# A hand-tuned list schedule made anew: another load pace, another bias between two engines, another set of nudges

## The chip, the cores and the metric

The kernel runs on one core of a Trainium2 chip. Its time is device microseconds of one execution; five executions of the kernel before took between 175.0 and 175.97 us, with a median of 175.41. The core has five engines that run side by side and wait for each other through semaphores: PE multiplies matrices into PSUM banks, DVE and ACT do elementwise work and empty the banks, POOL issues the loads, and SP issues stores, small copies and transposes by DMA.

## What is computed

Attention over four batches of eight heads, 768 positions and 64 columns a head, is followed by a gated long convolution over the same 512 channels:

```python
scores = scale * np.matmul(q, k.transpose(0, 1, 3, 2)) + bias   # local window of 96, 8 global keys
a = softmax(scores);  x = concat_heads(a @ v)                   # (4, 768, 512)
proj = x @ w_proj;  x1, x2, x3 = split(proj, 3)
x2_conv = irfft(rfft(x2) * rfft(filter_fft))                    # over the 768 positions
out = (x1 * x2_conv * x3) @ w_out                               # (4, 768, 512) float32
```

## The kernel before

Each batch goes through two halves. In the attention half, q and k tiles are transposed on PE (`transposes`, or `transpose_pair` for batch 0), `scores` multiplies them for a pair of heads, ACT takes the exponential, DVE multiplies by a mask, `values` multiplies by v, DVE divides by the row sums (the tile `xn`), and `transpose_x` brings the result to `xT` with channels on partitions. For batch 3, q and k are transposed by DMA on SP instead (the set `CROSS`). In the convolution half, `butterfly` forms sums on DVE, `conv` projects them on PE (L1168) into `ab`, `forward` transforms them (L921) into `X`, DVE multiplies by the filter's spectrum (`prod`, `sums`), and PE transforms back (L1190, L1193) into `eo`. `mixed` and `gated` on DVE make `y` from it and from `gate` (L1107, which multiplies `xT` by the outer columns of `w_proj`), and `project` (L1224) multiplies by `w_out`; the tile `ot` is stored. Attention of batch b+1 runs beside the convolution of batch b.

The code does not write the order of the work by hand. Every operation is recorded in a `Plan` with its cost in microseconds per engine, the values that it reads and writes, and the PSUM banks that it takes. `lay` then walks a clock of its own: at each step it takes, among the operations that are ready, the one that can start first, with a rank that decides between near ties. The rank is the operation's due time in its batch plus a nudge from the list `NUDGES`, which holds two numbers for each operation in the order of recording: the first is added to the rank (hundredths), the second to a lean (thousandths). Where an operation may run on ACT or on DVE, it goes to the engine on which it would end first, with `FAVOUR` plus the lean added on DVE's side. Copies that empty a PSUM bank (`evac`, `copy`, `times`) have this choice; masks, `prod`, `mixed` and `gated` are DVE's alone, exponentials ACT's.

Loads are costed in two parts: the issue on POOL, from the count of packets (L581), and the transfer, which the plan sends through a serial queue of POOL loads, `n * cost / 16` for n packets, so that a later load lands after all earlier ones. `load_run` loads the value tiles of batch 0, one DMA per tile; `load_rows`, `load_q` and `load_v` load those of the other batches.

Where PE would stand still, `fill` puts matmuls on a zero tile (`busy`, L561). `program` at last hands each engine its operations in the planned order. Each engine then runs its own list in that order and waits where an input is not there. The plan's times are gone by then: only the order and the choice of engine remain.

Of the kernel before, what the change touches and what calls it, by code (L numbers as in the profile page):

```python
# [16 lines left out]
P = 128  # L17
NG = 8
KL = P - NG
# [45 lines left out]
class Plan:  # L65
# [90 lines left out]
    def lay(self):  # L156
# [84 lines left out]
        20941, -23817, 24195, -7663, -15997, -12768, 0, 6867, 24904, -5965, 0, -17644, -7477, -5060, -24645,  # L241
        7853, -19816, -5063, -21771, 2690, -43764, -11197, -12559, 13745, -25952, 704, 42886, 22331, -9503,
        -5990, 1975, -8514, 0, -4745, 0, -11122, 0, -4678, 0, -2503, 0, 2703, 49094, -5453, 12582, 138, 0,
        2677, 0, -19674, 0, 1176, -15359, 22897, 0, -11534, 10311, -526, -2410, -3266, -17322, 33944, 3602,
        1512, -259, 8045, -40045, 7265, 30354, -27115, -43002, 18207, -23341, -7539, -18530, 19032, 26814,
        -11634, -11666, 14102, -46374, 23798, -33916, -1835, -50116, 19804, 11572, 3115, -29987, 8167,
        28348, 11218, -36506, -4010, 22595, 36152, -34543, -29090, 14477, 8599, -2614, 27869, 0, -7546, 0,
        -16680, 0, -17125, 0, -13816, 0, -16742, 0, -14791, 0, 16347, 0, 25926, 0, -5843, 0, 4323, 0, 10329,
        0, -15463, 0, 18719, 19536, 1819, 15033, -8513, 19843, -16154, 22937, -10325, 10268, 18083, 28464,
        -245, 36921, 25314, 18091, 23717, 29990, 35772, 38801, 14920, -6087, 48142, 8522, 52890, 26449,  # L250
        9945, 19818, 13034, -4027, 31031, 38806, 4230, 41538, 37058, 57207, 5161, 73250, 47340, 15138, 7448,
        7588, -18862, -23184, 16201, 32855, -3461, -31158, 19212, 17292, -17171, -42089, 23948, -22897,
        41474, 22968, 9803, 20589, 17748, 27185, 9614, -12894, 18131, 34936, 25299, 8438, 6083, -14729,
        -6326, 20819, -4821, -45272, 14951, 23049, 18994, 19751, 14180, 9780, 8132, -5251, 30597, 5195,
        -13743, -20605, 22464, -8378, 9715, -15388, 24239, 30711, -28388, -18939, -10787, -61348, 4309,
        -55267, -13, 1094, 47816, -21137, 19514, -30248, 2935, -8278, -9837, -18023, -6570, 60379, 10396,
        -16481, -3595, 36204, 6725, 7341, 2733, -6320, 2309, -25178, -24402, -13811, 32179, -16072, 9119,
        -2714, 7410, 3663, 9827, -12105, 12955, -28897, -10780, 51012, 14628, 1754, -22401, 13485, -3085,
        -4184, -21186, 36085, 6397, -8855, 31954, -12447, -8150, 15733, -13896, 5026, 16795, 39884, -2708,
        -12411, 41445, 7799, -26420, -28275, -1112, 280, 15059, -34598, 7843, 11808, -2433, -42337, -15655,  # L260
        -82713, -26014, -2215, 17107, -16388, 8416, -5143, -482, 11676, 33336, -33050, -14302, -15709, 144,
        -40429, 16554, 20320, -15285, -23321, -23667, -37185, -1273, -54080, -28453, -27659, 6317, -22336,
        19053, 19920, -9468, 13332, 22411, 27116, 4391, -74445, 3023, -18681, -23979, -41613, 4865, 40148,
        7658, 30769, -27204, 74556, 7934, 45890, 33096, 13491, -38443, -29399, 22140, -31839, 3648, 16007,
        9481, -16106, 20874, 29238, 150, 21929, 13455, 55399, 11501, -15951, 23586, -26638, -4060, 43304,
        -15855, -14976, -24332, -29525, 11042, -20570, 17346, -12584, -16297, -2377, 13286, -4899, -10436,
        -16741, -11712, -11582, 3253, -26673, 7977, -2469, -30454, -20346, 4897, -20954, -22758, -46710,
        10239, -64392, 12875, 21717, 11446, -5702, -21422, -30610, 8795, -40918, -18411, -67424, -18195,
        -69743, -37254, -9433, 5562, -19751, -18453, -71731, -18388, -70805, -1711, -10582, -11961, -23871,
        -19336, -40186, 22987, -5316, -14258, -16870, -14629, -15256, -1521, -23735, -47928, 16443, 10761,  # L270
        54821, -14436, 72922, 14379, 51678, -16015, 7320, -29070, 46924, -8772, 32829, -16584, 31588, -6267,
        34457, 3590, -31558, 24732, -10923, -14504, 32964, 8385, 5143, 36919, -32728, 25956, -14039, 11349,
        4986, 12927, 31546, 37533, -59658, -3559, 18051, 38808, 73841, -2119, 50706, 31457, 23261, -6025,
        -10079, 16467, 30400, 21292, 8455, 18584, -31806, 7305, 57789, 8768, 50111, 13745, -35470, -3712,
        41732, 25577, 24126, 19787, 8533, -937, 21590, 18777, 39119, 2282, -20749, -8396, 12672, 28818,
        16646, -10937, 11614, -10567, -21879, 2676, 18819, 31186, 4639, -15944, 16046, -32624, -29674, 1458,
        -9769, 13249, 0, 5375, 0, 1092, 0, 12535, 0, -19918, 0, 7960, 29554, -1962, 0, -31760, -168, -6234,
        32766, -9812, 0, -10387, 0, -9046, 0, -15969, 0, -982, 0, 14749, 0, 3802, 0, -1279, 0, 787, 0,
        24394, 0, 585, 0, -8398, 0, -11228, 0, 3326, 0, 6490, 0, 8805, -9920, 48938, 4735, 3905, -8205,
        -7191, -2044, 30228, 9924, 17307, 44468, -7542, -13358, -26667, -32913, -1805, -12682, 11399, 4538,  # L280
        3723, -22628, -3325, -5518, -17717, -21936, -17617, 10761, 26253, 20517, 7433, -4870, 28624, 25658,
        19340, 26925, -2699, 6125, 1356, -32310, 4183, -34292, 9989, -301, 1810, -17428, 15687, 23847,
        -22689, 26981, -20480, 46983, 12123, 9766, -4520, -746, 28862, 34014, 10760, 6990, 8399, -5341,
        -15584, 1444, -14598, -73642, 3303, 13007, 8220, -28684, 28385, 13493, 24628, -45198, -17244,
        -10136, 9475, -47887, -7547, 7854, 3939, -42446, 4154, 6812, 8242, -48704, -1611, -63875, 33975,
        -7810, -11179, -28621, 16046, -44155, 9482, 11839, 816, 25833, -4109, -14570, -12788, -4638, -2226,
        38013, -10513, -15011, -22283, -13043, -4434, 42230, -3028, 22311, -8443, -17844, 235, 18709, 7407,
        694, 17699, -24403, -29271, 4023, 6438, 43047, 1961, -12567, -29992, -8533, -4997, 40320, 27143,
        -1596, 11862, -21869, 8088, 32138, 44960, -6503, 17127, -15964, -21900, 21021, 59471, -34643, 12523,
        -54582, -1316, 4600, 20558, -6800, 9656, -21248, 21127, -32577, -23524, -12065, 10079, 7711, 11366,  # L290
        -17248, 26917, -25081, 12272, -16114, 12346, -3728, -4335, 21426, -10974, -27771, -20579, -13097,
        17282, -13589, -356, 22677, -15422, -10715, -12729, -34376, 2982, -20468, 11300, 2568, 7069, -5522,
        31878, -34399, -7695, 40664, -13553, -2045, -23324, -3339, -14404, -30632, -16381, -30178, 40050,
        -5959, -18941, 65029, -12040, 5363, 12421, -38116, -914, -35103, -4066, -4341, -20161, 26164,
        -21963, -9873, 21957, -2405, -6671, -20834, -12785, -47639, 27815, -8119, -1028, -4099, -31470,
        -45086, -17747, -56282, -14506, -37669, -8628, -5599, -35946, 1030, -12669, -35647, -2384, -32701,
        5577, 11677, -18878, 19540, -2288, -3689, 3395, -22559, -3163, -53669, -13281, 12767, -23778, 2008,
        -11131, 17587, -6082, -27729, 3930, -34024, 15838, 7012, -4139, 5154, -18748, -10652, -14438,
        -38218, -7406, -27281, 3651, 8333, 2357, 4397, -10262, -10115, 15008, -19298, -2425, -4559, 12746,
        -19302, -12587, 20081, 15257, -15456, -670, -12979, -20565, -7481, -4642, 9549, -23538, 42477, 921,  # L300
        -33191, 5231, 23254, -26129, -25207, -20621, -36661, 31925, -8000, 22268, -22467, -11797, -11838,
        -23754, -59344, 27973, -19506, -27508, -61395, 25876, 15950, -5301, -31395, -19472, 15820, -2929,
        -1351, -4676, 11568, -5649, 12795, -20002, 15116, -21404, -1438, 419, 26641, 2392, -5098, -775,
# [83 lines left out]
        -47616, 6427, 4471, 18429, -13169, 10884, -52679, -25140, 13532, 17369, 12295, -1454, 22421, -26080,  # L387
        22521, 13223, -4166, 12199, -22498, 6019, 50773, -19701, 32853, 1141,
    )
    FAVOUR = 0.0  # L390

    def fill(self, out):

# [75 lines left out]
class Fused:  # L469
# [458 lines left out]
    def transposes(self, what, t, src, cols):  # L928

        nc, g = self.nc, self.g  # L930
        b = g.bank()
# [494 lines left out]
```

## Time and profile before

| | |
|---|---|
| median of five executions | 175.41 us |
| profiled execution, span and own time | 173.2 us, 175.0 us |
| PE busy | 163.6 us, 1727 matmuls, 27 of them fillers |
| DVE, ACT busy | 148.7 us, 149.8 us |
| POOL busy | 75.5 us, all before 88 us |
| clock granted to PE | 1.00 throughout |
| first matmul of the values | 16.93 us, the second 17.67 us |
| last matmuls (outputs) start | 164.03 us |

The span runs from the first to the last instruction; the profiled execution's own time lies 1.8 us above it. In a row of the timeline the first number is the start, the second the time from the start of the first to the end of the last instruction merged into it; the part in brackets is how long the engine stood idle before it, and for what. The busy time of a matmul includes its way through the array, so that neighbours overlap: sixteen matmuls of 384 columns take 2.60 us from one start to the next group's, while each is shown as 0.33.

### The profile page before, as it was taken

The numbers are of one execution on the slowest core, as the hardware profiler recorded it, in microseconds if no ns is written. First come the engines' busy times: TensorE is split into PE (matmuls) and PEld (weight loads), VectorE is DVE, ScalarE is ACT, GpSimd is POOL, SyncE is SP. The second block draws the span as 40 slices with busy tenths as digits, with TensorE's granted clock in tenths as the row PEclk, the third lists the DMA queues.
The fourth block names the chain that finished last, engine by engine and source line by source line (L and its number), as shares of the span: only waits on it lengthen the run. The fifth ranks groups of instructions, "written<-read, shape, count | busy, mean of one in ns | idle before, by whom it ended". The sixth has DMA issues, their size and how long they took to land.

```text
span 173.2 us, 4484 instructions
## 1 busy us (share of the span) xinstructions
PE 163.6 (94%) x1727; PEld 101.7 (59%) x1727; DVE 148.7 (86%) x360; ACT 149.8 (86%) x298; POOL 75.5 (44%) x97
## 2 busy tenths in 40 slices
PE   7798999978999999999999999999999999999991
PEld 2376767645445656876445667754556784466540
DVE  6543869889999987999998999899999999999930
ACT  7999997976999986999998996889999797878761
POOL 7999777287997998799920000000000000000000
PEclk9999999999999999999999999999999999999999
DMA  6999999999999999999999994300431000040354
GB/s 180 159 126 124 112 184 207 188 153 151 138 148 167 150 154 149 114 143 151 142 128 93 364 149 95 61 0 0 192 114 62 4 0 2 0 184 2 140 222 185
DMA packets 86997, 21.82 MB, mean 126 GB/s; under 512 B 77616, under 2 KB 84032, under 8 KB 86976
## 3 DMA queue, kind: packets, MB, share of 16 engines
q0 software_dynamic: 75408, 12.47, 111.0%
q1 hardware_dynamic: 11568, 9.07, 19.8%
q8 instruction: 13, 0.21, 0.5%
q14 instruction: 8, 0.07, 0.1%
HBM read 25.69 MB, written 6.29 MB: 185 GB/s over the span
## 4 chain that ended last, share of the span: by engine, by line
PE 72%; DMA 13%; POOL 5%; DVE 4%; ACT 3%; issue 1%; POOLq 0%; ACTq 0%
PE bank L1107 19%; PE bank L1224 12%; PE bank L1168 12%; DMA qn<-in_q_dram 9%; PE bank L921 6%; PE bank L1190 5%; PE bank L984 5%; DMA vn<-in_v_dram 4%; PE bank L1069 3%; PE bank L1024 3%; PE bank L935 3%; PE bank L1029 2%; ACT E L999 2%; DVE xn L1048 2%; POOL kn L581 1%
## 5 line engine op out<-in xcount | busy, mean ns | idle before, releaser
L1107 PE MATMUL bank<-xT,w 128*128 128x384 f16 x256 | 45.7, 326 | 0.0
L999 ACT ACTIVATE E<-bank 128x864 f16<-128x864 f32 x48 | 41.3, 933 | 0.7 <-PE bank L984 0.6
L1107 PEld LDWEIGHTS <-w 128*128 128x128 f16 x256 | 24.1, 98 | 15.4 <-issue 0.8
L581 POOL DMA_DIRECT2D vn<-in_v_dram x29 | 26.6, 934 | 1.7 <-DMA w<-in_moe_w_proj_dram 1.7
L581 POOL DMA_DIRECT2D kn<-in_k_dram x24 | 21.9, 923 | 2.0 <-PE bank L935 1.3
L1224 PE MATMUL bank<-wo,y 128*128 128x512 f16 (+1 forms) x100 | 22.2, 371 | 0.0
L1006 DVE TENSOR_TENSOR E<-E,mask 128x864 f16<-128x864 f16 x36 | 21.3, 597 | 0.4 <-ACT E L999 0.4
L581 POOL DMA_DIRECT2D qn<-in_q_dram x21 | 18.4, 882 | 6.3 <-PE bank L1107 3.8
L1117 ACT CAST g<-bank 128x384 f16<-128x384 f32 x32 | 15.6, 488 | 4.1 <-PE bank L1107 3.3
L1048 DVE TENSOR_TENSOR xn<-bank,rc 128x512 f16<-128x512 f32 (+1 forms) x24 | 18.3, 771 | 0.3
L569 ACT ACTIVATE ot<-bank 128x512 f32<-128x512 f32 (+1 forms) x24 | 14.4, 625 | 3.8 <-PE bank L1224 3.6
L569 ACT ACTIVATE x<-bank 128x384 f16<-128x384 f32 x27 | 13.6, 506 | 3.5 <-PE bank L1107 2.6
L1024 PE MATMUL bank<-vn,E 128*128 128x65 f16 x224 | 15.6, 193 | 0.5 <-DMA vn<-in_v_dram 0.5
L569 ACT ACTIVATE ab<-bank 128x512 f16<-128x512 f32 x23 | 13.9, 636 | 2.2 <-PE bank L1168 2.2
L1024 PEld LDWEIGHTS <-E 128*128 128x128 f16 x224 | 14.2, 97 | 2.8 <-DMA vn<-vn 0.5
L1224 PEld LDWEIGHTS <-y 128*128 128x128 f16 x100 | 9.5, 98 | 10.0 <-DVE y L1266 0.2
L1029 PE MATMUL bank<-vn,E 128*128 128x65 f16 x192 | 15.2, 193 | 0.0
L984 PE MATMUL bank<-QT,KT 64*128 64x216 f16 (+2 forms) x224 | 14.9, 241 | 0.3 <-DVE xn L1048 0.3
L1029 PEld LDWEIGHTS <-E 128*128 128x128 f16 x192 | 13.2, 97 | 0.7 <-issue 0.3
L565 ACT CAST eo<-bank 128x384 f16<-128x384 f32 x30 | 12.2, 522 | 0.3 <-PE bank L1193 0.3
L984 PEld LDWEIGHTS <-KT 64*128 64x128 f16 x224 | 8.4, 94 | 6.9 <-issue 4.5
L565 ACT CAST X<-bank 128x512 f16<-128x512 f32 x21 | 12.2, 631 | 0.0
(144 smaller groups left out, 337.0 us busy)
## 6 DMA issues: line engine op xcount, KB each, us to landing
out_dram<-ot SPq DMA_DIRECT2D x23, 256.0 KB
vn<-in_v_dram POOLq DMA_DIRECT2D x28, 120.0 KB, 7.2
kn<-in_k_dram POOLq DMA_DIRECT2D x21, 120.0 KB, 6.4
qn<-in_q_dram POOLq DMA_DIRECT2D x18, 128.0 KB, 6.9
w<-in_moe_w_proj_dram POOLq DMA_DIRECT2D x4, 256.0 KB, 8.6
g<-in_moe_filter_fft_dram POOLq DMA_DIRECT2D x1, 768.0 KB, 13.1
qn<-in_q_dram POOLq DMA_DIRECT2D x3, 192.0 KB, 4.0
kn<-in_k_dram POOLq DMA_DIRECT2D x3, 192.0 KB, 4.5
```

Source lines behind the costliest of these rows:

```text
L565: {"A": nc.scalar.copy, "V": nc.vector.tensor_copy, "G": nc.gpsimd.tensor_copy}[e](out, in_)
L569: self.nc.scalar.mul(out, in_, c)
L581: return self.g.op(eng, 0.57 + 0.00035 * nbytes[0] if eng == "G" else 0.5, lambda _: e.dma_start(dst, src), w=w, r=r, nbytes=nbytes, name= ...
L984: nc.tensor.matmul(bs[hh].f32()[:, off:off + w], self.KT[hs, hp, P * m:P * m + P], self.QT[hs, hp, KL * m:KL * m + w], start=(off == 0 and ...
L999: g.op("A", act(864), lambda _: nc.scalar.activation(eo, bs[0].two()[:, :, 0:432].rearrange("p h (m w) -> p h m w", m=2), Act.Exp, scale=s ...
L1006: g.op("V", dve(864, 2), lambda _: nc.vector.tensor_mul(eo, eo, mk), r=[("E", hp, gi), ("mask", hp)], w=[("E", hp, gi)], name="masked")
L1024: nc.tensor.matmul(o[:, n, hh], ef[:, at:at + P], vt[:, t, 2 * hp + hh, :], start=first, stop=(t == 0), skip_group_check=True)
L1029: nc.tensor.matmul(o[:, n, hh], ef[:, at:at + P], vt[:, t - 1, 2 * hp + hh, :], start=False, stop=True, skip_group_check=True)
L1048: nc.vector.tensor_mul(to, o[:, :, :, 0:D], rc.to_broadcast([P, 2, 2 * nt, D]))
L1107: nc.tensor.matmul(bk.f32()[:, 0:h], self.w[:, c, o + P * j:o + P * j + P], self.xT[:, c, h * s:h * s + h], start=(c == 0), stop=(c == 3))
L1168: nc.tensor.matmul(bk.f32(), src[:, c], w[:, c, DM:2 * DM], start=(c == 0), stop=(c == 3))
L1224: nc.tensor.matmul(bk.f32()[:, 0:n], y[:, c, P * t:P * t + P], self.wo[:, c, cs], start=(c == 0), stop=(c == 3))
```

## The change

Four edits:

- `NUDGES` is replaced as a whole, and `FAVOUR` goes from 0.0 to -0.1, which makes DVE look 0.1 us quicker in each choice between ACT and DVE.
- In `load_run`, the value tiles of batch 0 count 1200 packets in the plan's transfer queue instead of 960 (8 heads times 120 rows).
- In `load`, the issue cost on POOL is computed from at most 1024 packets.
- `transposes` takes the batch, and the copy of the global key columns spans seven tiles less those of that batch in `CROSS`.

None of these changes what is computed. All reach the chip only through the order on each engine and the choice between ACT and DVE.

```diff
     NUDGES = (
-        20941, -23817, 24195, -7663, -15997, -12768, 0, 6867, 24904, -5965, 0, -17644, -7477, -5060, -24645,
...
     )
-    FAVOUR = 0.0
+    FAVOUR = -0.1
...
-        return self.g.op(eng, 0.57 + 0.00035 * nbytes[0] if eng == "G" else 0.5, lambda _: e.dma_start(dst, src),
+        return self.g.op(eng, 0.57 + 0.00035 * min(nbytes[0], 1024) if eng == "G" else 0.5, lambda _: e.dma_start(dst, src),
                          w=w, r=r, nbytes=nbytes, name=name, bias=-2000.0 + self.loads)
...
         self.load("G", dst[NG:P, t:t + n, :, 0:self.D], rows, [what + (i,) for i in range(t, t + n)],
-                  (8 * KL * n, 256), f"load{what}{t}")
+                  (1200 * n, 256), f"load{what}{t}")
...
-    def transposes(self, what, t, src, cols):
+    def transposes(self, batch, what, t, src, cols):
...
         if what == "k" and t == 0:
-            kv = self.KT.rearrange("p i (t c) -> p i t c", t=7)
+            n = 7 - sum((batch, "k", i) in self.CROSS for i in range(7))
+            kv = self.KT.rearrange("p i (t c) -> p i t c", t=7)[:, :, 0:n]
             g.op("V", dve(224), lambda _: self.copy(
-                "V", kv[:, :, :, 0:NG], kv[:, :, 0:1, NG:2 * NG].to_broadcast([P, 4, 7, NG])),
+                "V", kv[:, :, :, 0:NG], kv[:, :, 0:1, NG:2 * NG].to_broadcast([P, 4, n, NG])),
...
-            self.transposes(what, t, src, cols)
+            self.transposes(b, what, t, src, cols)
```

## The prediction

> **What bounds the kernel now.** I read the page first, then the chain of waits, the waits by engine, the timeline of PE where it waits, and the busy times by stretch. The page's busy times and slices (40 slices of 4.33 us; DMA rows left out):
>
> ```profile
> PE 163.6 (94%) x1727; PEld 101.7 (59%) x1727; DVE 148.7 (86%) x360; ACT 149.8 (86%) x298; POOL 75.5 (44%) x97
> PE   7798999978999999999999999999999999999991
> DVE  6543869889999987999998999899999999999930
> ACT  7999997976999986999998996889999797878761
> PEclk9999999999999999999999999999999999999999
> ```
>
> PE is full from about slice 17 (70 us) to the end, at an undiminished clock, so after 70 us no order can win time there; it can only lose some. What can be won lies before 70 us. The waits of PE, longest first:
>
> ```profile
> PE bank L935 <- DMA kn<-in_k_dram: 1.2, 1, 1.2
> ...
> PE bank L1024 <- DMA vn<-in_v_dram: 0.5, 1, 0.5
> PE bank L1069 <- DVE xn L1048: 0.4, 2, 0.3
> PE bank L935 <- DMA qn<-in_q_dram: 0.4, 1, 0.4
> ```
>
> The wait that the title speaks of, first values on v's tile, is the second line, 0.5 us. The larger one is the first: the transposes of batch 1's k. PE's timeline there (start, duration, line, tiles, count, idle before):
>
> ```profile
> 34.03 2.76 PE L1107 MATMUL bank<-xT,w 128*128 128x384 f16 x16
> 36.63 0.39 PE L935 MATMUL bank<-ident,qn 128*128 128x128 f16 x4
> 36.85 0.81 PE L1107 MATMUL bank<-xT,w 128*128 128x384 f16 x4
> 37.50 0.39 PE L935 MATMUL bank<-ident,qn 128*128 128x128 f16 x4
> 39.11 0.62 PE L935 MATMUL bank<-ident,kn 128*128 128x128 f16 x8 [1.23 <-DMA kn<-in_k_dram]
> 39.57 2.11 PE L1107 MATMUL bank<-xT,w 128*128 128x384 f16 x12
> 41.52 0.39 PE L935 MATMUL bank<-ident,qn 128*128 128x128 f16 x4
> 42.28 0.40 PE L935 MATMUL bank<-ident,qn 128*128 128x128 f16 x4 [0.38 <-DMA qn<-in_q_dram]
> 42.52 1.03 PE L1168 MATMUL bank<-w,xo 128*128 128x512 f16 x4
> ```
>
> PE stood 1.23 us for k while twelve gate matmuls that needed nothing from that DMA were queued behind. The busy times by stretch (PE, PEld, DVE, ACT, POOL) show who else is near its limit:
>
> ```profile
> 40.00:50.00 10.00, 9.62 (x74) 4.55 (x72) 9.57 (x24) 8.69 (x14) 9.05 (x11) 1.00 2.49 145
> 50.00:60.00 10.00, 9.53 (x129) 5.56 (x129) 9.63 (x27) 9.81 (x18) 8.99 (x11) 1.00 2.06 157
> 60.00:70.00 10.00, 9.67 (x125) 6.42 (x122) 8.07 (x19) 7.85 (x16) 8.74 (x10) 1.00 2.45 151
> 110.00:160.00 50.00, 50.00 (x443) 29.95 (x441) 49.44 (x102) 43.79 (x85) 0.00 (x0) 1.00 0.13 49
> ```
>
> DVE is 96% busy from 40 to 60 and 99% from 110 to 160: a second bound directly under PE.
>
> **The change part by part.** The sum is made against the profiled execution, 175.0 us: a span of 173.2 and 1.8 around it. The median of the five runs is 175.41, so 0.4 is added at the end.
>
> *First value tiles.* In the changed kernel's order, the first value group stands behind the same six score groups and the same three transposes as before, with five filler matmuls (L561) ahead of it for three. POOL issues the same loads in the same order up to batch 3, so v's tile lands at 17.67 as before. Fillers began at 16.28, three of them ended the stretch at 16.93 (0.217 each); five end at 17.36. The wait only shrinks: 0. If a filler overran, +0.2; no gain below 0, since the tile is no earlier. The four score groups of pairs 2 and 3 still follow the first values, so for this place the change does not do what its title says.
>
> *The clock of the plan.* Each of the seven first value tiles now counts 1200 packets instead of 960, and FAVOUR and all nudges are new, so the whole order is. Since the plan's DMA queue is serial, every later load is due later in it, batch 1's q and k too. The order shows it: all 32 gate matmuls of the second half now stand before the first k transpose, and three projections (xr, xcf, xo) after k and two q. Before, from 34.03 to 42.52, PE did 32 gate matmuls (2.60 us for 16: 5.20) and six transposes of four (0.22 each: 1.33), 6.53 of work in 8.49: 1.96 lost. After, gates, three transposes and three projections of 0.86 come to 5.20 + 0.66 + 2.59 = 8.45, with k wanted at 39.23, when it has landed (39.11). The projections want DVE's last xr: before it ended at 40.74, behind a wait of 1.31 for ACT's inverse table; after, that table copy stands behind four sums and DVE should be done by 39.5 to 40.8. So PE gains 1.96 less 0 to 1.0: I take -1.7; ends -2.0 and -0.7.
>
> *Before the gates.* Values of pairs 2, 3 move ahead of the last score group, DVE's xn and with it the last xT before the gates (now DVE, 0.40, for ACT, 0.60) come earlier; before, gates began at 27.23 on an xT that ended at 27.18. Taken -0.2; from -0.6 (the xn's wait of 0.6 for the exps gone) to +0.5 (DVE's 0.8 of mask copies stand ahead of that xT).
>
> *From 42 to 70 us.* Score visits fall from ten to seven; a visit costs 0.11 beside its matmuls (0.97 against 0.86 for the projection that follows scores): -0.3. Against it, conv 0's products now precede the last xn of batch 1 on DVE, and the inverse precedes batch 2's transposes on PE. PE's own work up to the first inverse group takes it there near 64 us; DVE's list up to the last product adds up to 53.9 us, each operation at the time from its start to the next start that its form shows here. Before, the same count stood at 50.4 when the clock said 66.4, 16.0 behind, of which 1.31, 0.39 and 1.89 were waits that the new order can avoid; 12.4 to 16.0 behind gives 66.3 to 69.9. So PE will wait on DVE there, and part of the front's gain goes: taken +0.7, between -0.5 (waits on xn of 0.2 to 0.5, which PE had before, gone) and +2.5. POOL's waits for free q and k tiles are covered: batch 2's loads of q start at 48.80, and PE has read batch 1's first q by 43. SP has three of batch 3's transposes ahead of batch 0's outputs, as before; POOL issues one v tile of batch 3 two q tiles (0.9 each) earlier, 20 us ahead of its use: 0.
>
> *Copies moved between ACT and DVE.* On DVE: five xT, two eo, two ab, two whole ot and one cast more; one xn, two KT, two QT, one X, one x, two near and half an ot fewer. By the means of their rows +6.6 and -4.8: +1.8 us on DVE in all. Up to batch 1's outputs DVE has more, in the last third about 1 us less to do; there it is the cover that PE needs. Taken +0.2; ends -0.5 and +1.8.
>
> One xn of batch 3 goes from one DVE operation (0.93) to twelve on ACT, a form without a row. The nearest is the slope's sixteen 64x64 scalings in 3.27, 0.204 each: 2.45. The 128x48 masks at 0.329 would give 3.95; no less than the 0.93. Sixteen gate matmuls (2.60) cover 2.45; after that PE stands: taken +0.1, ends 0 and +1.4.
>
> *No effect.* The copy of the global columns keeps its seven tiles: the set that it counts holds batch 3 alone, whose tiles SP transposes. The issue cost only tells the plan 0.93 for 0.91.
>
> *Tail.* 28 output matmuls and the last ot as before, about 3.7 us after the last matmul; the last two half evacuations are both ACT's, at 0.38 within PE's 0.43 each: 0, up to +0.5 as the eight gates now stand in one run before the last outputs.
>
> Two rules speak against it. DVE's f32 evacuations took 0.684 where ACT's took 0.636, but its f16 copies of 576 columns 0.454 against 0.646. The Trainium skill ("Perfetto Trace Analysis", Optimizing Scalar/DVE Operations) gives DVE about 74 ns more access time on PSUM per instruction than ScalarE; on some eight net evacuations that would be an estimated 0.6 us more on DVE, which the f16 row denies.
>
> POOL issued v's tiles at 0.906 each from 10.09 to 16.43, with DVE half idle, and at 0.935 from 38.69, with DVE full. The skill's "SBUF — State Buffer" (two separate sides) says some DVE modes lock GpSimd out wholly while it writes descriptors; by that 1.8 us more DVE work could delay loads as much, by the rows 0.03 per load.
>
> Sum: 0 - 1.7 - 0.2 - 0.3 + 0.7 + 0.2 + 0.1 + 0 = -1.2. 175.0 - 1.2 = 173.8 for such an execution, 174.2 as median.
>
> **Rivals.** *DVE takes over (slower).* Place: the inverse of batch 0 and the products after it. If DVE's idle time stays what it was (173.2 - 148.7 = 24.5), its +1.8 goes straight to the end: 177.2 at the most, 176.2 if the last third gives its 1 us back. It decides once DVE reaches the last product of conv 0 later than 69 us. For it: 99% busy late on; against: 3.6 us of its early waits have other work in front now.
>
> *The gain is given back (no change).* PE comes 1.7 ahead to 42 us and waits as long for DVE's products: 175.4. For it: the +2.5 end above. Against: PE lost 1.4 us by rows of waits from 40 to 70 before too.
>
> *All kept (much faster).* The front gives -2.0 - 0.6 and nothing new waits: 172.7. For it: 110 to 160 us had no wait of PE even with DVE at 99%.
>
> *The title's wait alone.* Only the 0.5 at 17.67 goes: 174.9. Against: that tile lands when it did.
>
> **How the numbers follow.** About 0.3% (0.5 us) is what a measurement here can tell from nothing. Forecast 0.45; DVE takes over 0.24; given back 0.14; all kept 0.12; title alone 0.05. Faster: 0.40 of the forecast's chance (174.9 and less), all kept, half of the title's: 0.55. Same: 0.05 of the forecast, 0.10 of given back, the rest of the title's: 0.17. Slower 0.28. The forecast's own range is 173.2 to 175.2; to hold eight in ten the range takes in most of all kept and DVE takes over: 172.7 to 176.7.
>
> **What would show it.** Right: no PE wait on k near 39 us, the first L1168 at 40 us ahead of the first scores, PE's wait before the first inverse group on DVE under 2.5 us; DVE's busy time near 150.5. Wrong: the front's gates not ready at 33.5 (then the k wait stays), a PE wait on DVE over 2.5 us between 60 and 70, or new waits after 110 us.

## The result, and where the profile changed

The changed kernel takes 174.2 us (median of 54 executions, 172.69 to 176.23) against 174.9 us for the kernel before (94 executions, 173.83 to 178.29). The ratio is 0.9952 with a 95% interval of 0.9939 to 0.9966: by the ratio 0.84 us faster, between 0.59 and 1.07. Medians and ranges here hold every execution; ratios and intervals leave out those more than 1.5% above the fastest of their kernel. The forecast's 174.2 was 1.2 us below a profile of 175.0, with a median of 175.41 for the kernel before. The profiled execution took 174.68 us, with a span of 172.9.

The page of the changed kernel (busy times, and the span in 40 slices):

```profile
PE 164.6 (95%) x1727; PEld 102.5 (59%) x1727; DVE 151.3 (87%) x362; ACT 150.3 (87%) x307; POOL 74.9 (43%) x97
...
PE   7997989999989999999999999999999999999991
```

DVE has 2.5 us more to do than before (151.3 against 148.7), PE one more (the same matmuls, counted with their way through the array). The slices of PE have no long gap, as before. The waits of PE, from the list of waits (total, times, longest):

```profile
PE bank L628 <- DMA kn<-in_k_dram: 1.0, 1, 1.0
...
PE bank L985 <- DVE KT L565: 0.5, 2, 0.3
PE bank L1025 <- DMA vn<-in_v_dram: 0.3, 1, 0.3
PE bank L985 <- ACT E L1000: 0.3, 1, 0.3
```

The wait of 1.23 us for batch 1's k and that of 0.38 for its q are gone. A new one of 1.0 us, for k of batch 0 at 16.25, has come near the start. The timeline of PE at the place where the k wait had been:

```profile
35.25 5.36 PE L1108 MATMUL bank<-xT,w 128*128 128x384 f16 x32
40.45 0.39 PE L935 MATMUL bank<-ident,kn 128*128 128x128 f16 x4
40.67 0.61 PE L935 MATMUL bank<-ident,qn 128*128 128x128 f16 x8
41.12 1.03 PE L1169 MATMUL bank<-w,xr 128*128 128x512 f16 x4
...
43.71 0.39 PE L935 MATMUL bank<-ident,kn 128*128 128x128 f16 x4
...
45.56 0.36 PE L985 MATMUL bank<-QT,KT 64*128 64x216 f16 x4
```

All 32 gate matmuls stand in one run, then one k tile and two q tiles, then three projections, with no gap up to the first scores. That is the order that the prediction read. But the run of gates began at 35.25; before, it began at 34.03. The busy times by stretch (PE, PEld, DVE, ACT, POOL):

```profile
40.00:50.00 10.00, 9.27 (x85) 5.39 (x84) 9.93 (x24) 9.09 (x14) 9.15 (x11) 1.00 2.28 140
50.00:60.00 10.00, 9.78 (x119) 5.58 (x119) 10.00 (x26) 8.85 (x17) 9.11 (x11) 1.00 2.10 156
60.00:70.00 10.00, 9.69 (x97) 6.48 (x94) 9.74 (x25) 9.91 (x21) 9.10 (x11) 1.00 2.88 142
110.00:160.00 50.00, 50.00 (x434) 29.84 (x435) 48.99 (x100) 44.88 (x95) 0.00 (x0) 1.00 0.16 59
```

From 60 to 70 us DVE is busy for 9.74 where it had 8.07 before, and ACT for 9.91 where it had 7.85. From 110 to 160 nothing of note has changed: PE is full, DVE at 98%.

To compare kernels whose orders differ, the sections below use the time that PE has lost up to a point: the clock, less the matmuls issued up to there, each at the pace that its form holds where nothing waits (0.216 us for 512 columns, 0.1625 for 384, 0.055 for 128, 0.03 for a value matmul). Small fixed costs are in it, so only differences between kernels count, and these to about 0.2 us. Each row is one execution; the last column is the ratio of the kernel's runs.

| execution | at 22 us | 34 | 43 | 90 | time against before |
|---|---|---|---|---|---|
| before | 6.89 | 8.18 | 10.19 | 16.10 | 1 |
| changed | 7.59 | 9.14 | 9.46 | 15.83 | 0.9952 |
| changed, second profile | 6.59 | 7.84 | 7.85 | 14.60 | 0.9956 |
| gates first | 6.87 | 8.19 | 9.70 | 15.89 | 1.0016 |
| scores first | 7.19 | 8.44 | 9.73 | 16.94 | 1.0001 |
| window 34 to 46 | 6.88 | 8.15 | 8.15 | 15.64 | 0.9989 |
| before up to 34 | 7.04 | 8.28 | 8.49 | 15.26 | 0.9925 |
| changed up to 34 | 6.70 | 8.21 | 9.51 | 16.75 | 1.0066 |
| before up to 42 | 6.88 | 8.15 | 9.25 | 16.24 | 1.0059 |
| gates behind | 6.59 | 8.27 | 8.38 | 15.67 | 0.9992 |
| engines of before | 6.59 | 8.48 | 9.69 | 18.29 | 1.0271 |

### The profile page after: what moved, and what is told of

Read it like the earlier page. It is cut to its first block, busy times and chain, and to the rows that moved or that the text cites. A ratio compares the mean times of both kernels' runs of the same rounds, so it can differ in the third digit from the quotient of the medians.

```text
span 172.9 us, 4500 instructions
## 1 busy us (share of the span) xinstructions
PE 164.6 (95%) x1727; PEld 102.5 (59%) x1727; DVE 151.3 (87%) x362; ACT 150.3 (87%) x307; POOL 74.9 (43%) x97
## 4 chain that ended last, share of the span: by engine, by line
PE 67%; DVE 18%; POOL 5%; DMA 4%; issue 2%; ACT 1%; POOLq 0%
PE bank L1108 19%; PE bank L1225 12%; PE bank L1169 9%; PE bank L1191 5%; DMA vn<-in_v_dram 4%; PE bank L985 4%; PE bank L921 4%; PE bank L1025 4%; PE bank L1070 3%; PE bank L1030 3%; DVE E L1007 2%; DVE xn L1049 1%; PE bank L976 1%; DVE g L1120 1%; PE bank L935 1%
## 5 line engine op out<-in xcount | busy, mean ns | idle before, releaser
L1108 PE MATMUL bank<-xT,w 128*128 128x384 f16 x256 | 44.1, 326 | 0.0
L1000 ACT ACTIVATE E<-bank 128x864 f16<-128x864 f32 x48 | 39.9, 905 | 3.3 <-PE bank L985 3.2
L581 POOL DMA_DIRECT2D vn<-in_v_dram x29 | 26.1, 918 | 1.7 <-DMA w<-in_moe_w_proj_dram 1.6
L1007 DVE TENSOR_TENSOR E<-E,mask 128x864 f16<-128x864 f16 x36 | 20.1, 591 | 0.3 <-ACT E L1000 0.3
L1049 DVE TENSOR_TENSOR xn<-bank,rc 128x512 f16<-128x512 f32 (+1 forms) x23 | 17.3, 760 | 0.3
L569 ACT ACTIVATE ot<-bank 128x512 f32<-128x512 f32 (+1 forms) x23 | 12.8, 591 | 5.0 <-PE bank L1225 5.0
L1025 PE MATMUL bank<-vn,E 128*128 128x65 f16 x224 | 15.9, 193 | 1.1 <-issue 0.5
L569 ACT ACTIVATE x<-bank 128x384 f16<-128x384 f32 x28 | 14.3, 522 | 2.7 <-PE bank L1108 2.3
L1030 PE MATMUL bank<-vn,E 128*128 128x65 f16 x192 | 15.5, 193 | 0.0
L569 ACT ACTIVATE ab<-bank 128x512 f16<-128x512 f32 x21 | 12.5, 618 | 1.9 <-PE bank L1169 1.5
```

The source lines that it names most:

```text
L569: self.nc.scalar.mul(out, in_, c)
L581: return self.g.op(eng, 0.57 + 0.00035 * min(nbytes[0], 1024) if eng == "G" else 0.5, lambda _: e.dma_start(dst, src), w=w, r=r, nbytes=nb ...
L1000: g.op("A", act(864), lambda _: nc.scalar.activation(eo, bs[0].two()[:, :, 0:432].rearrange("p h (m w) -> p h m w", m=2), Act.Exp, scale=s ...
L1007: g.op("V", dve(864, 2), lambda _: nc.vector.tensor_mul(eo, eo, mk), r=[("E", hp, gi), ("mask", hp)], w=[("E", hp, gi)], name="masked")
L1025: nc.tensor.matmul(o[:, n, hh], ef[:, at:at + P], vt[:, t, 2 * hp + hh, :], start=first, stop=(t == 0), skip_group_check=True)
L1030: nc.tensor.matmul(o[:, n, hh], ef[:, at:at + P], vt[:, t - 1, 2 * hp + hh, :], start=False, stop=True, skip_group_check=True)
```

## The experiments

The first theory was the prediction's: the change wins the k wait, on PE, between 34 and 43 us, and loses about 1 us in front. Its rivals were that DVE takes the gain back, and that the gain comes from another part of the order. In the kernels below an order is edited after the plan has made it; what is computed stays the same.

### Before, with the gates first

```diff
-        return self.program(self.fill(self.lay()))
+        return self.program(self.moved(self.fill(self.lay())))
...
+        for steps, behind in (((355, 359, 361, 364), 188), ((356, 360, 362, 363, 365), 186)):
...
```

Four transposes (q, q, k, k) go behind the last gate, and the copies that empty their banks behind a gate's copy.

> The kernel before with one move: the four transposes of batch 1's q and k that stood among the gate matmuls, and the copies that empty their banks, go behind the last gate. Theory (the wait of 1.23 us for k, and 0.38 for q, is what the change wins on PE): those waits go and the time falls by 1.0 to 1.6 us. Rival (the gain is given back at DVE's products before the first inverse): the waits go and the time stays within 0.4 us. Rival (the gain of the change comes from the rest of its order): the same, nothing here.

175.37 us against 174.98, ratio 1.0016 (0.9988 to 1.0044): nothing won. The k wait at 39 did go. PE's timeline in this kernel:

```profile
39.18 0.61 PE L943 MATMUL bank<-ident,qn 128*128 128x128 f16 x8
39.63 0.61 PE L943 MATMUL bank<-ident,kn 128*128 128x128 f16 x8
41.16 0.73 PE L943 MATMUL bank<-ident,qn 128*128 128x128 f16 x8 [0.92 <-DVE QT L573]
...
44.85 0.40 PE L943 MATMUL bank<-ident,kn 128*128 128x128 f16 x4 [0.61 <-DMA kn<-in_k_dram]
```

The four transposes run from 39.18 without a gap. Then PE waits 0.92 for DVE's copy of q, 1.5 us later, and 0.61 for the next k tile. The lead over the kernel before was 1.44 us at 40 us (8.19 lost against 9.63) and 0.01 at 46 (10.82 against 10.83). The theory that the k wait is worth its length fell here.

### Before, with the scores ahead of the first values

```diff
...
+        for steps, behind in (((128, 129, 130), 122),):
...
```

The first value group, its reciprocal and its scaling go behind the second score group.

> The kernel before with the move that the change's title speaks of, and nothing else: the first value group, its reciprocal and its scaling go behind the first two score groups of head pairs 2 and 3, so that these no longer queue behind a value tile in flight. Theory (these scores could not have started earlier: the copies of their keys ended on DVE at 17.99 us, when the values were done too): the wait on v's tile of 0.54 us turns into a wait on DVE, time within 0.2 us. Rival (the title's wait is worth its length): 0.4 to 0.6 us faster.

175.15 against 174.98, ratio 1.0001 (0.9974 to 1.0028). The move that the prediction calls the title's is worth nothing at this place. The expectation had the time right and the reason in part. The scores did start earlier, at 17.59 for 18.31; their part that reads the keys started at 18.03, just when DVE's last copy of the keys ended (18.03). PE then waited for DVE two groups later:

```profile
17.59 0.54 PE L983 MATMUL bank<-near,slope 64*128 64x432 bf16 x4
...
20.43 0.55 PE L983 MATMUL bank<-near,slope 64*128 64x216 bf16 x8 [0.36 <-DVE xn L1056]
```

The other executions show the same from the other side. In four with the front of the kernel before (before, gates first, window, before up to 42) PE had lost between 5.76 and 6.30 us at 18.5 us, as the value tile came sooner or later, and at 22 us 6.87 to 6.89 in all four; in a fifth, with a wait of 0.84 on v, it was 6.51 and then 7.04. Most of what is won or lost on v is gone 4 us later.

### Splices at the first gate

In the first, the changed kernel takes its steps up to the first gate from the kernel before, in the second the other way round.

```diff
-        return self.program(self.fill(self.lay()))
+        return self.program(self.fronted(self.fill(self.lay())))
+
+    FRONT = (
+        (0, "V"), (12, "S"), (5, "G"), (11, "V"), (1, "V"), (16, "G"), (10, "V"), (14, "S"), (2, "A"),
...
```

`FRONT` lists the other kernel's steps up to its first gate, with their engines; shown is its start in the first splice.

> The changed kernel, but with the steps up to the first gate matmul taken, with their order and engines, from the kernel before. Theory (what the change wins lies behind the first gates, about 1.8 us there, and its front gives about 1 us back): the gates start near 27.2 us instead of 28.4, and the time falls by 1.4 to 2.0 us against the kernel before, to about 173.1. Rival (the later start is absorbed further on, because DVE and not PE sets the pace behind it): no faster than the changed kernel, -0.6 to -1.0 against the kernel before.

> The kernel before, but with the steps up to the first gate matmul taken from the changed kernel. Theory (the changed front costs about 1 us): gates near 28.4 us and the time up by 0.5 to 1.2 us; part of the delay may disappear in the wait for batch 1's k, whose loads are no earlier, which is why the low end is 0.5. Rival (the late gates of the changed kernel are chance of one profiled execution, or are absorbed): within 0.3 us of the kernel before.

175.61 (ratio 1.0025, 0.9992 to 1.0057) and 178.04 (1.0166, 1.0116 to 1.0216). Neither theory had such numbers, and the traces show that the seam made them: PE stood 1.03 us at the first gates of the one, for DVE's `rc`, and 2.19 us at those of the other:

```profile
29.43 2.76 PE L1151 MATMUL bank<-xT,w 128*128 128x384 f16 x16 [2.19 <-DVE xn L1092]
```

At that seam the kernel before has a scaling (`xn`) and three small operations done, the changed kernel a reciprocal (`rc`) in their stead, and in the splices the gates meet DVE's missing steps. These two runs say nothing on the question, apart from one thing: the 2.0 us that the second had lost more than the kernel before at 34 (10.17 against 8.18) were still 1.94 at 90 us (18.04 against 16.10). In this run, time lost by PE ahead of 34 us was not made good behind.

### Splices at 34 us

At the second half's first gate the two orders have done the same work on PE, and differ in ten steps elsewhere, five of them butterfly sums that DVE has done in the kernel before and has still to do in the changed one.

```diff
-        return self.program(self.fill(self.lay()))
+        return self.program(self.replay(self.STEPS))
...
```

`STEPS` is a whole order, written out. "Before up to 34" has the first 213 steps of the kernel before and then the rest as the changed kernel orders it; "changed up to 34" has the first 205 of the changed kernel and then the rest as before; "window 34 to 46" has the 213, then the changed order up to 46 us of the plan's clock, then the rest as before.

> All steps of the kernel before up to its ninth gate group (near 34 us), then all remaining steps as the changed kernel has them. At this seam the two kernels differ by few steps, none of them on PE. Theory (PE's idle time behind 34 us is what the change wins, 11.5 before against 10.2 us after, and the changed front loses 1.0 us): 1.0 to 1.6 us faster than the kernel before, 0.4 to 0.9 faster than the changed kernel. Rival (the front's loss is chance of one execution): the time of the changed kernel, 0.6 to 1.0 faster than before. Rival (the changed kernel's front is what makes its rest possible): no faster than before.

> The mirror image: the changed kernel's steps up to its ninth gate group, then the remaining steps as the kernel before has them, with its transposes of k among the gates. Theory: PE loses 1.0 us in front and nothing is won behind, 0.6 to 1.2 us slower than before. Rival (front's loss is chance): within 0.3 us of before. Rival (the front carries the gain): faster than before.

> The kernel before with one window of the changed kernel's order: from the ninth gate group to plan time 46 us, so that all gates and then three projections and two transforms come ahead of the first scores of batch 1; in front and behind, the order of the kernel before. Theory (gates first wins only together with PE work that needs neither k nor DVE's next copy, here the projections): PE loses 0.6 us between 34 and 46 instead of 2.65, and most of it is kept, 1.0 to 2.0 us faster. Rival (what is won by 46 us is given back on the way to 70, as after the bare move of the gates): within 0.4 us of before.

> The changed kernel once more, for a second profile and times beside those of the spliced kernels. If the front's loss belongs to the order, PE again waits 0.9 to 1.0 us for the fourth pair of k near 15.3 us, and the gates start near 28.4 us. If it is chance, that wait is under 0.3 us or absent and the gates start by 27.7 us. Time 0.6 to 1.0 us below the kernel before in either case.

All beside the same runs of the kernel before (174.79):

| kernel | median | ratio | 95% interval |
|---|---|---|---|
| before up to 34 | 173.88 | 0.9925 | 0.9895 to 0.9955 |
| changed up to 34 | 175.98 | 1.0066 | 1.004 to 1.0092 |
| window 34 to 46 | 174.89 | 0.9989 | 0.9969 to 1.001 |
| changed, again | 174.13 | 0.9956 | 0.9931 to 0.998 |

Three things follow. The changed order from 34 us on is worth 1.3 us with the front of the kernel before. Its window up to 46 us alone, with the run of gates and the three projections, and 2.0 us of lead at 43 (8.15 against 10.19; against 9.25 in an execution with a shorter k wait it is 1.1), is worth next to nothing (0.2 us, with an interval that holds zero). And the changed front costs: 1.15 us with the rest of before, 0.25 by the medians (0.54 by the ratios) with the changed rest, where the intervals overlap.

The busy times from 46 to 70 (PE, PEld, DVE, ACT, POOL) show where the window's lead went; first the kernel before, then with the window:

```profile
46.00:58.00 12.00, 11.84 (x123) 5.82 (x123) 11.83 (x30) 11.82 (x20) 10.99 (x14) 1.00 2.09 154
58.00:70.00 12.00, 11.36 (x153) 7.62 (x152) 9.84 (x25) 9.84 (x19) 10.74 (x12) 1.00 2.44 152
```

```profile
46.00:58.00 12.00, 10.15 (x118) 5.65 (x117) 11.54 (x28) 11.33 (x19) 10.57 (x12) 1.00 2.14 155
58.00:70.00 12.00, 11.47 (x155) 7.81 (x152) 9.87 (x25) 9.91 (x19) 10.20 (x13) 1.00 2.67 143
```

and with the changed order to the end ("before up to 34"):

```profile
46.00:58.00 12.00, 10.93 (x128) 6.06 (x127) 11.93 (x28) 10.75 (x17) 10.52 (x13) 1.00 2.13 156
58.00:70.00 12.00, 11.59 (x116) 7.71 (x114) 11.73 (x29) 11.78 (x24) 11.17 (x14) 1.00 2.55 140
```

From 46 to 58 us DVE and ACT are both full in the kernel before (11.83 and 11.82 of 12), and then each stands idle for 2.2 us from 58 to 70. A PE that comes earlier into the first stretch, with the order of before behind it, waits longer in it: its busy time falls from 11.84 to 10.15. The window's timeline shows for whom: 0.42 us at 47.39 and 0.85 at 49.88 for exponentials, and 0.46 at 53.11 for `h`, all of ACT, 1.73 together:

```profile
49.88 0.38 PE L1088 MATMUL bank<-pp,fwd 128*128 128x512 f16 x1 [0.85 <-ACT E L1167]
```

One rival stays open. At 34 us the two orders have done the same work on PE; at 46 they have not. The window has two transforms and their copies done that the kernel before does later, and an exponential and a mask still to do, so part of these waits can be the seam's. The changed order fills the second stretch instead (11.73 and 11.78). Most of the idle time in the kernel before is two waits for PE, on DVE's and on ACT's timeline:

```profile
66.17 0.23 DVE L1053 RECIPROCAL rc<-bank 128x12 f32<-128x12 f32 x1 [1.89 <-PE bank L1029]
```

```profile
67.45 1.09 ACT L569 ACTIVATE h<-bank 128x512 f16<-128x512 f32 x2 [1.52 <-PE bank L895]
```

DVE stood with a reciprocal of batch 1's values in front of conv 0's products. These ran at 67.31, though ACT had ended the second copy of X at 62.41 and DVE the scaling of h at 61.66. PE did gates and values meanwhile. In the changed kernel the products run ahead of that reciprocal (in its second profile from 59 to 66 us), and its wait is 0.34:

```profile
70.46 0.23 DVE L1054 RECIPROCAL rc<-bank 128x12 f32<-128x12 f32 x1 [0.34 <-PE bank L1030]
```

The second profile also corrects the first on the front. Its wait for k of batch 0 is

```profile
15.53 0.53 PE L628 MATMUL bank<-ident,kn 128*64 128x128 f16 x12 [0.25 <-DMA kn<-in_k_dram]
```

where the first profile had 0.97, and its gates start at 26.77 instead of 28.38. In three other kernels with that front they start at 27.36, 27.21 and 27.62, in the kernel before at 27.23. The gates that came 1.2 us late in the first profile were one execution's luck.

### Before up to 42, changed behind

```diff
+        return self.program(self.replay(self.STEPS))
...
```

`STEPS` has the first 276 steps of the kernel before and then the rest as the changed kernel orders it.

> The kernel before up to plan time 42 us, with its waits for k and q; all steps behind as the changed kernel has them. Theory (the changed order behind 42 us does not win by itself; it only keeps the lead that PE brings from the gates): PE starts that stretch 2 us later than in the splice at 34 us and ends no better than the kernel before, between -0.3 and +0.9 us. Rival (the order behind 42 us wins by itself, because it fills the stretch from 62 to 70 us where DVE waits 1.89 and ACT 1.52 us for PE): 0.8 to 1.4 us faster than before.

176.0 against 174.84, ratio 1.0059 (1.0032 to 1.0086): 1.0 us slower, just over the upper end of the theory, and the rival is out. Behind this head the changed order is slower than the old one. Three of the longest, from the list of PE's waits:

```profile
PE bank L1152 <- ACT E L1167: 0.6, 2, 0.4
PE bank L1088 <- ACT ab L736: 0.5, 1, 0.5
...
PE bank L1192 <- DVE xn L1216: 0.4, 1, 0.4
```

Two of these are for ACT. With the window, ACT is busy for 10.59 us from 34 to 46, here for 8.46 (and for 8.81 in the kernel before): the three early projections give it copies to do that here come later, beside the exponentials. That this is the cause fits the waits, and was not isolated. Here too the seam is not at a point of equal work: the head has first scores done that the changed order does later, and projections still to do, so what the seam itself costs is in the 1.0 us.

### The changed kernel with its gates behind k again

```diff
+        return self.program(self.moved(self.fill(self.lay())))
...
+        for steps, behind in (((189, 194, 183), 359), ((190, 191, 196, 185, 192, 197), 362)):
...
```

Three gate groups go behind the first k and q transposes, and what empties their banks behind k's copy.

> The changed kernel with one part undone: three of its second half's gate groups (12 matmuls) and what empties their banks go behind the first transposes of batch 1's k and q, so that PE again meets k in flight. Theory (the lead from the gates is what the change wins): PE waits 1.2 to 1.8 us for k near 37 us, nothing behind can fill it, and the time is 0.4 us above to 0.2 us below the kernel before, that is 0.6 to 1.2 above the changed kernel. Rival (DVE and ACT set the pace from 42 to 62 us, so a later PE is absorbed): 0.6 to 0.9 us below the kernel before, as the changed kernel.

174.5 us, ratio 0.9992 (0.9967 to 1.0017): the time is where the theory put it, 0.6 us above the changed kernel by the ratios (0.4 by the medians). The reason is not the expected one. No wait for k came back, because the tile that had been late in the kernel before is the second (it landed at 39.07 there, the first at 38.10), and the changed order uses that one only behind the projections. PE's longest waits are now

```profile
48.61 0.27 PE L993 MATMUL bank<-QT,KT 64*128 64x216 f16 x2 [0.73 <-DVE KT L573]
56.77 0.19 PE L1033 MATMUL bank<-vn,E 128*128 128x65 f16 x1 [0.59 <-DVE xn L1057]
```

0.2 and 0.4 us longer than in the second profile of the changed kernel. That DVE comes later there fits them; what makes it later was not isolated.

### The changed order with the engines of before

```diff
+        return self.program(self.replay(self.STEPS))
...
```

`STEPS` is the changed kernel's order; behind 34 us each copy runs on the engine (ACT or DVE) that it has in the kernel before.

> The changed kernel with its order, but behind 34 us every copy, scaling and evacuation runs on the engine (ACT or DVE) that it has in the kernel before; 47 of them change, the twelve-piece scaling of batch 3 goes back to DVE, and DVE is relieved of some 2 us in all. By the prediction's term for the moved copies: 0.2 us better than the changed kernel, 0.7 to 1.2 us faster than before. Rival (order and choice of engine belong together, since ACT's exponentials are as full as DVE from 46 to 58 us): slower than the changed kernel by 0.5 us or more, no faster than before.

179.88 us, ratio 1.0271 (1.0232 to 1.031): 5.6 us slower than the changed kernel. The relief did not come either; DVE is busy for 151.4 us there, as in the changed kernel (151.3 and 150.9). PE waits in many places where the changed kernel waits less or not at all:

```profile
PE bank L1151 <- DVE KT L731: 0.8, 1, 0.8
PE bank L1335 <- DVE xr L1261: 0.6, 2, 0.4
PE bank L1274 <- ACT xT L731: 0.5, 1, 0.5
PE bank L1391 <- DVE y L1433: 0.4, 1, 0.4
```

From 34 us on, the waits that its timeline lists (over 0.15 us) add up to 4.0 us, against 1.0 and 1.3 in the two profiles of the changed kernel. That is about half of the 5.6; the other half was not traced.

### The pace alone

```diff
-                  (8 * KL * n, 256), f"load{what}{t}")
+                  (1200 * n, 256), f"load{what}{t}")
```

> The kernel before with the one edit that its title names: 1200 for 960 packets a value tile in the plan, with its old nudges. The plan then orders everything anew, and its own clock ends at 182 instead of 170 us. Theory (pace and nudges only work together): slower than before by 3 us or more. Rival (the measured pace is what makes the order better): faster than before.

184.66 us, ratio 1.0567 (1.0508 to 1.0626): 9.9 us slower, as the theory had it: with the old nudges the new pace makes a worse order. The new nudges with the old pace were not run. The other three edits change nothing at all: with `FAVOUR` at 0.0, the old issue cost or the old span of seven tiles, the plan gives the changed kernel's order on every engine, step for step. The leans from `NUDGES` have a median size of 17 us where an engine can be chosen, so 0.1 never tips one.

## Why the prediction was right, and where its steps were wrong

The time came out as forecast (174.2), partly because the kernel before now has a median of 174.9 and not 175.41; the sum of -1.2 is 0.1 to 0.6 us more than the interval of the gain allows. But the steps that add up to it do not each hold, and that their errors cancel is luck.

*The clock of the plan, -1.7.* The reading of the order was right, and the waits on k and q went. The step failed in taking the wait's length as a gain. Moved alone, the gates won nothing (ratio 1.0016); with the projections, 0.2 us (0.9989, an interval that holds zero). Its size was off too: 1.23 us was the longest of the four executions that come to this place in this order and without a delayed front; the others waited 0.54, 0.58 and 0.34.

*From 42 to 70 us, +0.4.* The prediction priced this stretch as a loss beside the gain. It is +1.0 without the gain in front ("before up to 42") and -1.0 with it (173.88 for "before up to 34" less 174.89 for the window). So the two parts cannot be priced apart: PE's lead is lost with the old order behind it, and the new order is slower without the lead. How much of this belongs to the seams at 42 and 46 us, which do not lie at points of equal work, stays open. The details held better. DVE was to reach the last product of conv 0 between 66.3 and 69.9; it started at 67.10 in the first profile and at 65.87, ahead of that range, in the second. PE was to wait for it 0.7; it had other work, and the longest wait near there is 0.18 and 0.28 for a copy of k. The prediction did see that the wait of 1.89 us could be avoided, but counted it only as a term against a loss.

*Before the gates, -0.2.* On PE it is about zero: at 34 us the changed front has lost 9.14, 7.84, 8.21, 8.27 and 8.48 in five executions (8.39 in the mean), that of before 8.15 to 8.28 in five. What the front does cost seems to lie on DVE, five sums behind at 34 us: with the old rest, DVE was busy for 11.77 us from 34 to 46 where the kernel before had 10.24, PE waited 0.75 and 0.56 for it, and the time rose by 1.15. The prediction looked only at when the gates start. The run of 32 gates started at 35.25 and at 33.64 in the two profiles, after the 33.5 that the prediction names as a sign of being wrong, and the k wait was gone all the same: that sign was too strict.

*First value tiles, 0.* Right, and beyond the reason given: even where the scores go ahead and the wait ends, nothing is left of it.

*Copies moved, +0.2.* DVE's busy time rose by 2.5 us, against the 1.8 of the count. But the step took it as a load to be priced by itself. With the new order and the old choice of engine DVE is as busy (151.4), and the time 5.6 us longer. Choice and order were made together and cannot be priced apart.

*Twelve pieces on ACT, +0.1, and the tail, 0.* The twelve took 2.6 us, 0.22 each, against 2.45 from the slope's row, and PE has no wait near them. The last outputs show no wait either.

The two rules that spoke against the change did not decide it. The Trainium skill ("Perfetto Trace Analysis", Optimizing Scalar/DVE Operations) prices a DVE access to PSUM above ScalarE's; with 47 copies exchanged between the two, 24 off DVE and 23 onto it, the time rose by 5.6 us, which no price per copy gives; which queue has room when fits it, and was not isolated. The prediction's count of some eight net evacuations was too high: DVE reads a PSUM bank in 93 operations after and in 90 before. The lock-out of GpSimd that "SBUF — State Buffer" (two separate sides) describes would have to show in POOL's issues beside a full DVE, if DVE's operations there are of the kind that locks, which no row tells. In the changed kernel's profile POOL issued seven tiles of q, k and v from 49.39 to 55.69, 0.90 us each, with DVE busy for 11.93 of the 12 us from 46 to 58; with DVE half idle, seven of v took 0.906 each.

Of the rivals, "the gain is given back" is what happens to the gates' lead under the old order behind it, and its place was right. "DVE takes over" did not come: the last product started at 67.10 at the latest, under the 69 from which that rival was to decide. "All kept" adds up to 172.8 rather than 172.7 (175.4 less 2.6), which moves no conclusion. Why the changed order behind 42 us needs the lead was read from busy times and waits, and not isolated step by step.

## What to carry to other kernels

A removed wait on the bounding engine need not be worth its length: the engines behind it must be able to use the earlier start. Look at the next stretches. Here the lead of the wait removed alone was gone 6 us later, in waits for a copy of DVE and for the next k tile, and the window's lead in waits for ACT. Where a whole order is new, do not add the parts as if each stood alone; splice old and new at a point where both have done the same work, and run both crosses: at 34 us they gave -1.3 and +1.15 us here. The cuts at 42 and 46 us, where the work done differs, gave +1.0 and -0.2; they overlap, carry the cost of their seams, and are no parts of the -1.3. And take a DMA wait from several executions before it is put into a sum.

The splice of the old front with the changed rest (0.9925) beats the kernel before; beside the changed kernel in the same runs (0.9956) it is 0.25 us ahead by the medians, which the intervals do not separate.

## What was not expected of the hardware

The landing of the first loads scatters from execution to execution by a microsecond and more. In the same program, the changed kernel waited 0.97 us for k at 16 us in one profile and 0.25 in the other, with the issue on POOL within 0.02 us (9.59 and 9.61), and the first value tile was waited for 0.84 us in one execution with the front of the kernel before and not at all in another. Over all 14 profiles that load of k was issued between 9.38 and 9.61 us and landed between 13.20 and 16.20. Part of the scatter is absorbed by 22 us. A difference below 1 us in the first 30 us of two single profiles says nothing here.
